# Opening transfers in another order: the transform weights first, the first feed-forward matrix behind the reads of Z, the second one in quarters behind a later read

## The chip, the cores and the metric

The kernel runs on one core of a Trainium2 chip. The core has five engines that run side by side, each through its own list of instructions in order: TensorE (PE, matrix products), VectorE (DVE), ScalarE (ACT), GpSimd (POOL) and SyncE (SP). They wait for one another through semaphores. Copies between the chip's DRAM and the on-chip memory SBUF are carried by 16 DMA engines. An engine issues such a transfer as one instruction of its own list; in this kernel SP issues most of them, POOL issues the loads of `x` and of `moe_w_out`. The profile shows the transfers of SP as queue q1 (hardware_dynamic) and those of POOL as queue q0 (software_dynamic). The metric is the device time of one execution in microseconds (us); lower is better.

## The reference

A spectral layer over 8 sequences of 3008 positions and 256 features is followed by a feed-forward block on all 24064 rows:

```python
X = np.fft.rfft(x, axis=1)                    # x: 8 x 3008 x 256
Xr, Xi = X.real, X.imag
Yr = Xr @ w_r - Xi @ w_i + b_r                # w_r, w_i: 256 x 256
Yi = Xr @ w_i + Xi @ w_r + b_i
Yr = np.sign(Yr) * np.maximum(np.abs(Yr) - 0.01, 0.0)      # likewise Yi
y = np.fft.irfft(Yr + 1j * Yi, n=3008, axis=1)
h = y.reshape(-1, 256) @ moe_w_in             # 256 x 2048
g = np.where(h > 0.0, h, np.exp(np.minimum(h, 0.0)) - 1.0)
out = g @ moe_w_out                           # 2048 x 256
```

## The kernel before

A transform of length 3008 is done as two smaller ones, 47 and 64 points, in units named by letters. For one batch `b`:

- A (`unit_A`, 6 of them) multiplies the loaded `x` (three tiles `xt0` to `xt2`) by the matrix `M1` and stores the result to a DRAM buffer `DA`. `load_Z` reads `DA` back in another arrangement, as tile `Z`.
- X (`unit_X`, 8) multiplies `Z` by `M2` into `XT`.
- M (`m_group`, called by `unit_M` or, in the opening, `first_M`; 12) applies `w_r` and `w_i`, adds the bias and shrinks by 0.01. The weights were cast before, by four instructions on POOL, into `wcat_r` and `wcat_s`.
- B (`unit_B`, 6) goes back by `M3` and stores to a DRAM buffer `DB`. `load_Bs` reads that back as four tiles `Bs`.
- Y (`unit_Y`, 8) multiplies `Bs` by `M4` into `yT`.
- `front` and `back` are the feed-forward block: `front` multiplies by `w_in_s` into `hps`, ACT and DVE form the ELU into `gT`, and `back`, two steps later, multiplies by `w_out_r` into `ps_o`. One batch has 48 such steps, one step takes two of the 16 column blocks of `moe_w_in`, so eight steps in a row go through all of `moe_w_in` and `moe_w_out`.

The order of all instructions is written out by hand. The opening does batch 0 alone through A, X, M, B, with filler products (`idle_pe`) on TensorE; then come the A units of batch 1 and the first two Y units of batch 0. After that the main loop runs 384 steps, and `plan` puts the units of the next batches between the steps: in batch 0 the Y units 2 to 5 stand ahead of `front` in steps 1 to 4, and the X units of batch 1 from step 5 on. A unit that stands there ahead of `front` runs ahead of it in the order of TensorE too.

What the opening loads, and in which order, before the change:

- POOL issues the six loads of `x` for batch 0 (line 115) from the very start, between the instructions that build index tables.
- SP issues the six stores of `DA`, then `w_r` and `w_i` (lines 504 and 505), the four reads of `Z`, the two bias rows, and the first quarter of `moe_w_in` (`load_w_in(0)`, line 580; the transfer itself is line 564). That last one writes into memory that the constants' staging tiles (`stagep`, among them `w_r_f` and `w_i_f`) held until then, so it waits for the last reader of those.
- POOL, in its own list, casts the weights (lines 506 to 509), then runs `gate(Z_of[0][:, 8, 0:1])`. `gate` is a copy of one column into a small tile: it does nothing but make POOL wait until that part of its source has landed, and with it all that POOL issues later. Behind it stand the three loads of `x` for batch 1 and both halves of `moe_w_out` (lines 584 and 585, transfer line 569).
- SP's `load_w_in(1)`, `(2)` and `(3)` stand behind the stores of units B 0, 1 and 2 (lines 613, 617, 621).
- At the end of the opening SP issues `load_Bs(0, 0)` and `(0, 1)` (lines 635 and 636), which wait for all stores of `DB`; between the A units of batch 1 come their three stores of `DA` (line 156) and the other two reads of `Bs`; then the two reads of `Z` for batch 1 (line 655), which wait for those stores.

`scale_w_in` (lines 646 to 653) turns each quarter of `moe_w_in` into its bf16 form behind the opening, on DVE and ACT.

Of the kernel before, what the change touches and what calls it, by code (L numbers as in the profile page):

```python
# [29 lines left out]
def kernel(  # L30
# [11 lines left out]
    nc = tc.nc  # L42
    P = nc.NUM_PARTITIONS
# [6 lines left out]
    NFT = DFF // P  # L50
# [54 lines left out]
    Bs_of = {}  # L105
    yT_of = {}
    def load_x(b, ci, m0=0, m1=8):

        src = bass.AP(
            tensor=x.tensor,  # L110
            offset=x.offset + (b * S + 8 * ci + m0) * D,
            ap=[[N1 * D, N2], [(NJ - 1) * D, 2], [D, m1 - m0], [1, D]],
        )
        dst = xts[ci][:, m0:m1, :]
        nc.gpsimd.dma_start(dst, src.bitcast(F32R))
# [98 lines left out]
    def first_M(q, i, eng):  # L214

        ps = pre1.tile([P, 2 * D], F32, name="mps1", tag="mps1")
        yb, clip = m_group(0, q, i, ps[:])
        let_go()
        Y_ = Y_of[0, q][:, i, :]
        if eng is nc.scalar:  # L220
            nc.scalar.activation(clip[:], yb[:], AF.Relu, bias=lam_n[:])
            held.append((Y_, yb, clip))
        else:
            eng.tensor_scalar(clip[:], yb[:], LAM, -LAM, ALU.min, ALU.max)
            eng.tensor_tensor(Y_, yb[:], clip[:], ALU.subtract)
# [35 lines left out]
    def load_Bs(b, w):  # L261

        Bs = wk4.tile([4 * K1, 8, D], BF16, name="Bs", tag="Bs")
        dv = DB_of[b].rearrange("k (c h m) d -> (k c h) m d", c=2, h=2)
        nc.sync.dma_start(Bs[:], dv[:, 8 * w : 8 * w + 8, :])
        Bs_of[b, w] = Bs
# [32 lines left out]
    with tc.tile_pool(name="stagep", bufs=1) as stagep:  # L299
# [29 lines left out]
        def row(name, shape):  # L329
            return stagep.tile(shape, F32, name=name)  # L330
# [3 lines left out]
        w3, a3 = (wk2.tile([P, NV, N2], F32, name="A", tag="A") for _ in range(2))  # L334
        w_r_f = row("w_r_f", [P, 2, D])
        w_i_f = row("w_i_f", [P, 2, D])


        nc.scalar.activation(dume[:], busy[:, 0:1], AF.Sin, bias=0.0, scale=0.0)

# [145 lines left out]
        def fA(u):  # L486
            unit_A(0, u, alone=True)
            if u < 5:
                idle_pe(3)
# [11 lines left out]
        wraps(1)  # L501
        signs(0)
        fA(5)
        nc.sync.dma_start(w_r_f[:], w_r.rearrange("(c p) e -> p c e", p=P))
        nc.sync.dma_start(w_i_f[:], w_i.rearrange("(c p) e -> p c e", p=P))
        pool.tensor_copy(wcat_r[:, :, 0:D], w_r_f[:])
        pool.tensor_copy(wcat_r[:, :, D : 2 * D], w_i_f[:])
        pool.tensor_scalar(wcat_s[:, :, 0:D], w_i_f[:], -1.0, None, ALU.mult)
# [50 lines left out]
    def load_w_in(q):  # L559
        if q < 3:  # L560
            wf = late3.tile([P, 2, FQ], F32, name="w_in_f", tag="Et")
        else:
            wf = late2.tile([P, 2, FQ], F32, name="w_in_f", tag="osb")
        nc.sync.dma_start(wf[:], w_in_v[:, :, q * FQ : q * FQ + FQ])
        w_in_f.append(wf)

    def load_w_out(hh):
        hf = slice(hh * NFT // 2, (hh + 1) * NFT // 2)
        nc.gpsimd.dma_start(w_out_r[:, hf, :], w_out_v[:, hf, :])

    def gate(src):

        t = gatep.tile([P, 1], F32, name="gate", tag="gate")
        nc.gpsimd.tensor_copy(t[0 : src.shape[0], :], src)


    def fB(v, on_dve=False):
        unit_B(0, v, alone=True, on_dve=on_dve)

    load_w_in(0)  # L580
    gate(Z_of[0][:, 8, 0:1])
    for ci in range(3):
        load_x(1, ci)
    load_w_out(0)
    load_w_out(1)
    for u in range(8):
        unit_X(0, u, alone=True, on_dve=u in (1, 4, 7))
        if u == 1:
# [21 lines left out]
    first_M(1, 1, nc.scalar)  # L610
    first_M(2, 0, nc.gpsimd)
    fB(0)
    load_w_in(1)
    first_M(2, 1, nc.scalar)
    first_M(3, 0, nc.gpsimd)
    fB(1)
    load_w_in(2)
    first_M(3, 1, nc.scalar)
    first_M(4, 0, nc.gpsimd)
    fB(2)  # L620
    load_w_in(3)
    first_M(4, 1, nc.scalar)
    first_M(5, 0, nc.scalar)
    fB(3)
# [9 lines left out]
        )  # L634
    load_Bs(0, 0)
    load_Bs(0, 1)

    def scale_w_in(q, on_dve):
        dst = w_in_s[:, :, q * FQ : q * FQ + FQ]
        if on_dve:  # L640
            nc.vector.tensor_scalar_mul(dst, w_in_f[q][:], 2.0 / S)
        else:
            nc.scalar.activation(dst, w_in_f[q][:], AF.Copy, scale=2.0 / S)
# [232 lines left out]
```

## Time and profile before

| what | value |
|---|---|
| time, median of 3 runs | 930.38 us (930.08 to 931.6) |
| profiled execution, its own time | 931.51 us |
| its span, first to last instruction | 929.7 us |
| mean granted TensorE clock | 0.998 of full speed |
| TensorE busy | 909.2 us, 98% of the span |
| VectorE, ScalarE, GpSimd busy | 734.5, 710.7 and 267.9 us |
| share of the chain that ended last on TensorE | 75% |
| moved by DMA | 106.21 MB, 114 GB/s over the span |
| moved by DMA from 4 to 15 us of the span | 353 GB/s |

Times in the views are counted from the start of the span. "Busy" counts instructions that compute; a wait is charged to what released it. The chain that ended last is followed back from the last instruction: each piece is the work that released the next one. In the table of stretches each row gives, for each engine, its busy time and the number of its instructions, then the granted TensorE clock, the mean busy share of the 16 DMA engines (a share above 1 means that the packets of several queues overlapped) and the rate in GB/s. "SPq" and "POOLq" are the instructions with which SP and POOL issue transfers.

### The profile page before, as it was taken

What the parts mean: (1) busy time and instruction counts of PE and PEld (TensorE: products, weight loads), DVE (VectorE), ACT (ScalarE), POOL (GpSimd) and SP (SyncE); (2) the same over time, 40 slices, a digit from 0 to 9 for tenths busy, and PEclk for the clock granted to TensorE, in tenths of its full rate; (3) what the DMA queues carried; (4) which work ended last, traced back from release to release, by engine and by line L of the source; (5) the groups of instructions that cost most, each with busy time, mean ns of one, the idle gap of its engine ahead of it and who ended that gap; (6) DMA issues with size and microseconds to landing.
All of it is one profiled execution on the core that took longest, in us unless ns stands there. A gap on an engine that the chain in (4) does not pass through costs nothing.

```text
span 929.7 us, 16768 instructions
## 1 busy us (share of the span) xinstructions
PE 909.2 (98%) x6583; PEld 644.4 (69%) x6583; DVE 734.5 (79%) x863; ACT 710.7 (76%) x818; POOL 267.9 (29%) x352
## 2 busy tenths in 40 slices
PE   8879999999999999999999999999999999999997
PEld 3447677776677666776677766777667766677775
DVE  7868778877788767886778877887778876888997
ACT  6657887787878788688787878778787878676654
POOL 6801441133310431205412153113331043321332
PEclk9999999999999999999999999999999999999999
DMA  8984216621383224722166021752138002421011
GB/s 264 353 254 136 91 47 187 196 69 46 95 223 111 69 65 126 224 84 86 51 181 202 24 91 46 222 161 68 47 94 224 22 24 63 116 51 43 23 46 43
DMA packets 90655, 106.21 MB, mean 114 GB/s; under 512 B 5264, under 2 KB 81296, under 8 KB 87216
## 3 DMA queue, kind: packets, MB, share of 16 engines
q1 hardware_dynamic: 84320, 77.61, 29.8%
q0 software_dynamic: 5968, 27.26, 8.9%
q8 instruction: 51, 0.84, 0.4%
q10 hardware_dynamic: 288, 0.26, 0.1%
q14 instruction: 28, 0.23, 0.1%
HBM read 55.31 MB, written 49.81 MB: 113 GB/s over the span
## 4 chain that ended last, share of the span: by engine, by line
PE 75%; DVE 14%; DMA 4%; ACT 4%; issue 1%; SPq 1%; DVEq 0%; POOL 0%; ACTq 0%; POOLq 0%
PE ps_o L749 30%; PE hps L688 29%; PE mps L189 8%; DVE gT L713 8%; DVE Et L724 3%; PE bps L238 2%; PE aps L143 2%; PE xps L174 2%; DMA Z<-DA 2%; DVE gT L715 1%; PE yps L276 1%; ACT Et L701 1%; DMA DA<-A 1%; DVE Et L726 1%; DMA xt<-in_x_dram 1%
## 5 line engine op out<-in xcount | busy, mean ns | idle before, releaser
L749 PE MATMUL ps_o<-w_out_r,gT 128*128 128x256 f32 (+1 forms) x3072 | 485.8, 301 | 0.8 <-DVE gT L713 0.5
L749 PEld LDWEIGHTS ps_o<-w_out_r,gT 128*128 128x128 f32 (+1 forms) x3072 | 406.4, 186 | 65.5 <-DVE gT L713 14.4
L688 PE MATMUL hps<-yT,w_in_s 128*128 128x512 bf16 (+1 forms) x1536 | 390.5, 376 | 5.4 <-DVE gT L715 2.7
L701 ACT ACTIVATE Et<-hps 128x1024 f32<-128x1024 f32 (+1 forms) x299 | 301.4, 1008 | 84.4 <-PE hps L688 80.4
L713 DVE SCALAR_TENSOR_TENSOR gT<-Et,hps 128x1024 fp32r<-128x1024 f32 (+2 forms) x187 | 219.9, 1176 | 62.9 <-ACT Et L699 41.6
L715 DVE SCALAR_TENSOR_TENSOR gT<-hps,Et 128x1024 fp32r<-128x1024 f32 (+1 forms) x198 | 240.1, 1213 | 17.6 <-DVE Et L726 0.9
L688 PEld LDWEIGHTS <-w_in_s 128*128 128x128 bf16 x1536 | 131.8, 98 | 141.0 <-issue 24.0
L726 DVE TENSOR_SCALAR Et<-Et 128x1024 f32<-128x1024 f32 (+1 forms) x198 | 136.0, 687 | 58.0 <-ACT Et L701 51.4
L204 POOL TENSOR_SCALAR clip<-yb 128x512 f32<-128x512 f32 x84 | 51.7, 615 | 335.1 <-DVE yb L196 234.5
L724 POOL TENSOR_SCALAR Et<-Et 128x512 f32<-128x512 f32 (+1 forms) x102 | 64.3, 630 | 271.1 <-ACT Et L701 269.9
L698 ACT ACTIVATE Et<-hps 128x1024 f32<-128x1024 f32 x84 | 86.4, 1029 | 70.0 <-PE hps L688 70.0
L205 POOL TENSOR_TENSOR Y<-yb,clip 128x512 bf16<-128x512 f32 x84 | 107.3, 1278 | 7.0
L196 DVE TENSOR_TENSOR yb<-mps,bias_bc 128x512 f32<-128x512 f32 x96 | 65.7, 687 | 39.3 <-PE mps L189 32.4
L699 ACT ACTIVATE Et<-Et 128x1024 f32<-128x1024 f32 x84 | 88.8, 1058 | 2.7
L126 ACT CAST yT<-yps 128x752 bf16<-128x752 f32 x63 | 49.7, 788 | 13.4 <-PE yps L276 13.4
L126 ACT CAST XT<-xps 128x768 bf16<-128x768 f32 x61 | 49.1, 807 | 13.7 <-PE xps L174 13.7
L189 PE MATMUL mps<-wcat_r,XT 128*128 128x512 bf16 x192 | 58.1, 384 | 0.6 <-ACT XT L126 0.6
L189 PE MATMUL mps<-wcat_s,XT 128*128 128x512 bf16 x192 | 57.1, 379 | 0.0
L126 ACT CAST A<-aps 128x1024 bf16<-128x1024 f32 x45 | 45.5, 1013 | 14.3 <-PE aps L143 11.9
L724 DVE TENSOR_SCALAR Et<-Et 128x512 f32<-128x512 f32 (+1 forms) x102 | 55.6, 545 | 0.4 <-ACT Et L701 0.2
L189 PEld LDWEIGHTS <-XT 128*128 128x128 bf16 x384 | 30.3, 98 | 29.5 <-ACT XT L126 0.9
L763 ACT COPY osb<-ps_o 128x512 f32<-128x512 f32 x88 | 47.2, 587 | 2.8 <-PE ps_o L749 2.8
(103 smaller groups left out, 398.5 us busy)
## 6 DMA issues: line engine op xcount, KB each, us to landing
xt<-in_x_dram POOLq DMA_DIRECT2D x21, 1024.0 KB, 5.2
out_dram<-osb SPq DMA_DIRECT2D x158, 128.0 KB
Bs<-DB SPq DMA_DIRECT2D x32, 384.0 KB
DA<-A SPq DMA_DIRECT2D x21, 512.0 KB
DB<-Bz SPq DMA_DIRECT2D x21, 512.0 KB
Z<-DA SPq DMA_DIRECT2D x7, 1152.0 KB
Z<-DA SPq DMA_DIRECT2D x11, 384.0 KB
xt<-in_x_dram POOLq DMA_DIRECT2D x6, 512.0 KB, 6.4
```

What stands on the lines that cost most here:

```text
L126: nc.scalar.copy(dst, src)
L189: nc.tensor.matmul(ps, lhsT=XT[:, dt, c, o : o + P], rhs=wm[:, dt, :], start=(m == 0 and dt == 0), stop=(m == 1 and dt == 1),)
L205: nc.gpsimd.tensor_tensor(Y_of[b, q][:, i, :], yb[:], clip[:], ALU.subtract)
L688: nc.tensor.matmul(hps[:, s, 0:nb], lhsT=w_in_s[:, dt, ft * P : ft * P + P], rhs=yT[:, dt, bs : bs + nb], start=(dt == 0), stop=(dt == 1),)
L698: nc.scalar.activation(E_, hps[:, :, 0:nb], AF.Relu, scale=-1.0)
L699: nc.scalar.activation(E_, E_, AF.Exp, scale=-1.0)
L701: nc.scalar.activation(E_, hps[:, :, 0:nb], AF.Exp)
L713: nc.vector.scalar_tensor_tensor(o, e, -1.0, h, ALU.add, ALU.max)
L715: nc.vector.scalar_tensor_tensor(o, h, 0.0, e, ALU.max, ALU.add)
L724: eng.tensor_scalar(E_[:, s], E_[:, s], 1.0, 0.0, ALU.min, ALU.max)
L726: nc.vector.tensor_scalar(E_, E_, 1.0, -1.0, ALU.min, ALU.add)
L749: nc.tensor.matmul(po[q][0 : t1 - t0, i_ % 2, :], lhsT=gT[:, s, t0:t1], rhs=w_out_r[:, ft, :], start=(ft == 0 and i_ % 2 == 0), stop=(ft = ...
```

## The change

Four moves, all of them transfers; no computing instruction is added or taken away, except one `gate`.

1. `w_r` and `w_i` are issued by SP at the very top, ahead of the stores of `DA`. The four casts on POOL stay where they are in POOL's list.
2. All four quarters of `moe_w_in` are issued where only the first was: on SP, behind the reads of `Z` and the bias.
3. Both halves of `moe_w_out` leave their place behind the loads of `x` for batch 1. In their stead four quarters are issued by POOL behind a new `gate` on the first read of `Bs`, at the end of the opening.
4. Nothing stands any more between the stores of `DB` on SP.

```diff
         w_r_f = row("w_r_f", [P, 2, D])
         w_i_f = row("w_i_f", [P, 2, D])
-
+        nc.sync.dma_start(w_r_f[:], w_r.rearrange("(c p) e -> p c e", p=P))
+        nc.sync.dma_start(w_i_f[:], w_i.rearrange("(c p) e -> p c e", p=P))
...
         fA(5)
-        nc.sync.dma_start(w_r_f[:], w_r.rearrange("(c p) e -> p c e", p=P))
-        nc.sync.dma_start(w_i_f[:], w_i.rearrange("(c p) e -> p c e", p=P))
         pool.tensor_copy(wcat_r[:, :, 0:D], w_r_f[:])
...
     def load_w_out(hh):
-        hf = slice(hh * NFT // 2, (hh + 1) * NFT // 2)
+        hf = slice(hh * NFT // 4, (hh + 1) * NFT // 4)
         nc.gpsimd.dma_start(w_out_r[:, hf, :], w_out_v[:, hf, :])
...
-    load_w_in(0)
+    for q in range(4):
+        load_w_in(q)
     gate(Z_of[0][:, 8, 0:1])
     for ci in range(3):
         load_x(1, ci)
-    load_w_out(0)
-    load_w_out(1)
...
     fB(0)
-    load_w_in(1)
...
     fB(1)
-    load_w_in(2)
...
     fB(2)
-    load_w_in(3)
...
     load_Bs(0, 0)
     load_Bs(0, 1)
+    gate(Bs_of[0, 0][:, 0, 0:1])
+    for q in range(4):
+        load_w_out(q)
```

## The prediction

> **What bounds the kernel now.** I read the chain that ended last first. From 75 us on it is TensorE, step after step, to the end (the page: PE 75% of the chain, 98% busy), and no transfer of the opening is waited for there. So whatever the change does is decided by when TensorE gets through the first 75 us, and those I read from the same chain, piece by piece (start, length, what):
>
> ```profile
> 2.18 6.01 DMA xt<-in_x_dram
> 15.62 3.09 DMA DA<-A
> 19.66 5.80 DMA Z<-DA
> 48.78 4.03 DMA DB<-A
> 55.95 2.44 SPq L265
> 58.47 6.16 DMA DA<-A
> 65.07 10.00 DMA Z<-DA
> ```
>
> The opening hangs on transfers at both its ends: `x` in, `DA` out, `Z` in; then computing from 27 to 48 us; then `DB` out, SP's issues, batch 1's `DA` out and its `Z` in. The last piece ends at 75.07, where X unit 2 of batch 1 starts. The longest waits up to 80 us say the same:
>
> ```profile
> PE yps L276 <- DMA Bs<-DB: 2.2, 1, 2.2
> PE xps L174 <- DMA Z<-DA: 1.6, 3, 0.7
> ```
>
> Then SP's own list, for what each transfer stands behind:
>
> ```profile
> 16.02 0.55 SPq L504 DMA_DIRECT2D w_r_f<-in_w_r_dram  x1
> 24.61 0.38 SPq L564 DMA_DIRECT2D w_in_f<-in_moe_w_in_dram  x1
> 52.88 0.79 SPq L265 DMA_DIRECT2D Bs<-DB  x2
> 58.47 1.00 SPq L156 DMA_DIRECT2D DA<-A  x1
> 64.71 0.77 SPq L163 DMA_DIRECT2D Z<-DA  x2
> ```
>
> And the table of stretches, for what the DMA engines carry (last two columns: busy share, GB/s):
>
> ```profile
> 38.00:44.00 6.00, 6.00 (x45) 2.59 (x40) 5.25 (x9) 3.96 (x5) 5.57 (x6) 1.00 1.64 349
> 51.00:54.00 3.00, 3.00 (x13) 1.35 (x14) 2.56 (x4) 1.96 (x3) 0.00 (x0) 1.00 0.15 37
> 54.00:58.00 4.00, 1.56 (x20) 0.81 (x18) 1.13 (x2) 1.08 (x2) 0.00 (x0) 1.00 0.96 268
> 58.00:64.00 6.00, 4.36 (x25) 2.24 (x26) 2.86 (x4) 3.29 (x5) 0.00 (x0) 0.72 1.09 341
> 64.00:66.00 2.00, 2.00 (x21) 1.66 (x20) 1.66 (x3) 1.34 (x2) 0.00 (x0) 1.00 0.17 43
> 66.00:72.00 6.00, 6.00 (x56) 4.77 (x52) 5.42 (x6) 5.08 (x6) 0.00 (x0) 1.00 0.97 247
> ```
>
> The reader is to see that from 54 to 64 the DMA engines are full, and with what: four `Bs` of 0.39 MB and three `DA` of 0.52 MB, 3.14 MB; the rows give 4 x 268 + 6 x 341 = 3.12 MB. These ten microseconds lie on the chain. The change puts `moe_w_out` (2.10 MB) into them.
>
> **Move 1, `w_r` and `w_i` first.** Two SP issues (0.55 and 0.49 us) leave the stretch from 16.0 to 17.1, where SP waits anyway (until 18.71) for the last `DA`: removing them gives SP nothing. Their 0.52 MB stood behind that `DA` in the same queue; its 3.09 us may shorten by 0 to 0.4, I take 0. At the top SP is free from 0.7 us, and data starts about 1.1 us after an issue (`Bs`: issued 52.88, 37 GB/s until 54), so the weights flow from about 1.9. `x` starts at 2.5 and then paces all six A units: its loads land at 5.5, 8.2, 9.4, 10.8, 12.2 and 13.7 us, the A products start at 5.57, 8.23, 9.58, 10.93, 12.27 and 13.81. At the full 353 GB/s of the stretch from 4 to 15 us the weights are 1.5 us of DMA time; before 4 us only 134 GB/s run (2.5 to 4), so most of it fits into room that was empty. Bounds 0 and 1.5; I take 0.4, nearer the empty rows. The casts on POOL (0.93, 0.61, 3.09, 0.61 us; 19.45 to 24.58 now) may start at 13.1. Their user starts at 28.97 and waited for `XT`, so this gives nothing, and the index work on DVE beside which they now fall has 0.5 us or more to spare before `Z` lands (22.55).
>
> **Move 2, `moe_w_in`.** SP's first such issue waited until 24.61 for the casts; now it waits only for DVE's last staging read (22.65), and four issues (0.38 to 0.54 us each) go out where SP has nothing to do before 37.77. They stand behind the `Z` reads in the same queue. The loads of `x` for batch 1 leave POOL's gate at about 24.3, when the second `Z` lands, not 25.17: they may cost the last `Z` 0 to 0.4 us; I take 0, since its data were through about 1 us ahead of its landing at 26.97, and `x` needs as long from issue to data. 2.1 MB and 3.1 MB of `x` at 391 GB/s (28 to 37 us) end near 39 us. `moe_w_in` is read from 48.67, `x` from 47.34: both are in time.
>
> **Move 3a, the stores of `DB` are freed.** Now each stands among half-megabyte loads; the DMA engines run full (365 GB/s) from 44 to 51, and the last store takes 4.03 us. With the queue empty it takes about as long as the last `DA` of batch 0, equally 0.26 MB: 3.09. With 0.75 us at 349 GB/s for the bytes, 1.1 to the first byte and 1 to 1.6 behind the last one (data end near 51.2, landing 52.8), it is 2.85 to 3.45. Gain 0.6 to 1.2; I take 0.8. `Bs` is then issued at 52.88 + 0.4 - 0.8 = 52.5 and lands at 56.5 instead of 56.87.
>
> **Move 3b, `moe_w_out` in the full stretch.** POOL has nothing to do from 45.4 to 75, so the gate (0.18 to 0.49 us) and four issues (half of the 1.10 and 1.13 us of the halves) cost it nothing, and nothing else waits behind them. Data flow from about 57.8. By then SP's queue has moved 4.2 x 268 = 1.13 MB; 2.02 MB of `Bs` and `DA` are left, which before ended at 64.0. The nearest row for the two queues together is 38 to 44 us: 349 GB/s, and there `moe_w_out`'s rest and SP's `DB` and `moe_w_in` got about the same each. At equal shares 2.02 + 2.10 MB end together near 57.8 + 11.8 = 69.6, and `moe_w_out` displaces at most 2.10 / 349 = 6.0 us. If SP's queue kept four fifths, `DA` would be late by 1.3 us, `moe_w_out` would fill the nearly empty rows 64 to 66 and 72 to 75, and the rest would fall on `Z`: some 2 us in all. Bounds 2 and 6.0; near the equal share, with some of the end falling into the gap behind the last `DA`, I take 5.0. The `Z` reads follow only when the last `DA` has landed (64.63 now), so all of it goes on to X unit 2, which had no slack (it waited 0.7 us).
>
> A sentence beside it: the Trainium skill, DMA: Bandwidth & Descriptors, Anatomy of one DMA, fits a transfer issued from GpSimd as 2.0 us plus its bytes at 436 GB/s, which makes the 2.10 MB an estimated 4.8 us instead of 6.0 and the sum +4.4 instead of +4.6; no row of this trace with both queues busy is that fast (349).
>
> Is `moe_w_out` itself late? The first `back` runs at 64.46 and needs the first quarter, the third at 68.8 the second. At half of 349 the quarters land near 61.5, 64.5, 67.5 and 70.5; the last two are read later than 72. Hidden, with 2 us or more to spare.
>
> **Sum.** +0.4 (start) - 0.8 (`DB`) + 5.0 (`moe_w_out` before `Z`) = +4.6 us at X unit 2, and from there on TensorE carries it to the end. The profiled execution is 931.51 us (span 929.7 and 1.8 around it), so 936.1 against it; it lies 1.1 above the median of the runs, and against that median of 930.38 I forecast 935.0.
>
> **Rivals.**
>
> Faster, by the place of `moe_w_out` alone: it yields to SP's queue. For it: 64 to 66 and 72 to 75 us are nearly empty (43 and 14 GB/s) and could hold 0.6 + 1.0 MB; POOL's loads are issued later than the first two `Bs` and the first `DA`. Against it: from 38 to 44 the same matrix was not held back by SP's transfers. It decides where less than 0.4 / 5.0 of the matrix, 0.17 MB, moves ahead of the last `DA` or of `Z`. With the best ends of the other terms (start 0, `DA` -0.4, `DB` -1.2) it gives 1.6 to 2.5 us less: 928.3.
>
> Half hidden: SP keeps the larger share, the displacement is at its bound of 2, the sum +1.6, and the time 932.0. Only the four-to-one share that I have assumed speaks for it.
>
> Slower still: TensorE's clock falls a second time. In the row from 58.70 to 62.40 it was granted 0.55, after two waits of TensorE of 2.2 and 1.0 us. With the change TensorE comes to X unit 0 at about 69.5 and `Z`'s first part lands up to 5.2 us (64.71 to 69.92, no wait) behind an issue at 69.7, so it idles 3 to 5 us. The same 3.7 us at 0.55 cost 1.7; with the start at its bound (+1.1) it is +7.4, 937.8. Against it: the slow steps lie beneath the wait for `Z`'s second part. The Trainium skill, TensorE: Matmul & The Clock Gate, Part 1, has the clock halve after one idle window of about 3.4 us; by that rule the longer wait would be enough by itself, and here the two shorter waits sufficed already.
>
> **How the numbers follow.** Forecast (+2.5 to +6.5): 0.54. Slower still (+6.5 to +9): 0.12. Half hidden (0 to +2.5): 0.14, of which 0.08 above 0.2%. Faster rival: 0.20, of which 0.14 beyond 0.2%. Here 0.2% is 1.9 us, about what a measurement of this kernel can tell from no change. So slower 0.54 + 0.12 + 0.08 = 0.74, within 0.12, faster 0.14. The range leaves out most of the faster rival and the tail of the slowest: 930.3 to 938.5; the forecast's own range is 932.9 to 936.9.
>
> **What the profile after would show.** Start: the first A products at 5.6 to 6, the sixth at 14.2; much more, and the weights collide with `x`. `DB`: the last store lands about 3.1 us after its issue. The main step: rates near 350 GB/s from 58 to 69, the last `DA` landing at 69 to 70 instead of 64.6, the reads of `Z` issued there, TensorE waiting for `Z` ahead of two X units, X unit 2 at about 79.7. If the last `DA` lands by 65, the step on the shared DMA engines is wrong, and so is the forecast. A wait of TensorE on `w_out_r` would show that the quarters come too late, which I exclude.

## The result, and the profile after

| | before | changed |
|---|---|---|
| median on the same chip | 931.03 us (930.08 to 931.97) | 937.16 us (935.58 to 938.34) |
| ratio, 95% interval | | 1.0066 [1.0053, 1.0078] |
| profiled execution, its time | 931.51 us | 936.45 us |
| its span | 929.7 us | 934.7 us |
| X unit 2 of batch 1 starts at | 75.11 us | 79.83 us |
| from there to the end of the span | 854.6 us | 854.9 us |

The change makes the kernel slower by 6.1 us. Measured once more (e14 below), it came to 1.0076 [1.0064, 1.0087]. Everything is lost before X unit 2 of batch 1: in all 14 profiled executions of this study the way from there to the end of the span takes 854.6 to 855.0 us.

The chain that ended last, of the changed kernel, up to that point (start, length, what):

```profile
1.46 6.07 DMA xt<-in_x_dram
17.36 2.31 DMA DA<-A
20.60 6.43 DMA Z<-DA
56.08 2.66 SPq L265
58.84 12.04 DMA DA<-A
71.32 8.47 DMA Z<-DA
79.83 0.52 PE xps L174 x8
```

Against the chain of before: the last store of batch 1's `DA` took 6.16 us and now takes 12.04. The reads of `Z` behind it are shorter, 8.47 instead of 10.00. The wait for the last store of `DB` is no longer in the chain. SP's list and POOL's, of the changed kernel, show what stands beside that store:

```profile
53.13 0.79 SPq L265 DMA_DIRECT2D Bs<-DB  x2
58.84 1.17 SPq L156 DMA_DIRECT2D DA<-A  x1
70.96 1.72 SPq L163 DMA_DIRECT2D Z<-DA  x2
```

```profile
57.21 0.18 POOL L573 CAST gate<-Bs 96x1 f32<-96x1 bf16 x1 [10.22 <-DMA Bs<-DB]
57.34 3.09 POOL L568 DMA_DIRECT2D w_out_r<-in_moe_w_out_dram  x4
```

SP issues `Bs` and `DA` at nearly the same times as before (52.88 and 58.47), and `Z` 6.25 us later (64.71 before). In between stands `moe_w_out`. The table of stretches, changed kernel (last three columns: granted clock, busy share of the DMA engines, GB/s):

```profile
58.00:64.00 6.00, 3.44 (x28) 1.80 (x28) 3.54 (x5) 3.83 (x5) 2.42 (x4) 1.00 1.21 342
64.00:66.00 2.00, 0.30 (x2) 0.00 (x0) 1.75 (x2) 1.02 (x1) 0.00 (x0) 1.00 1.45 265
66.00:71.00 5.00, 4.22 (x24) 3.33 (x25) 1.31 (x2) 0.96 (x2) 0.00 (x0) 0.66 1.32 328
```

The DMA engines are full up to 71 instead of 64, and the rate is (6 x 342 + 2 x 265 + 5 x 328) / 13 = 325 GB/s. TensorE stands idle in the second row, and is granted less clock in the third. Its three longest waits in the first 100 us, changed kernel (us in total, times, longest):

```profile
PE xps L174 <- DMA Z<-DA: 3.0, 5, 1.0
PE ps_o L747 <- DMA w_out_r<-in_moe_w_out_dram: 2.5, 1, 2.5
PE aps L143 <- DMA xt<-in_x_dram: 2.2, 1, 2.2
```

Of the 3.0 us in the first line 1.5 are waits for batch 1's `Z`, 0.9 ahead of X unit 0 and 0.6 ahead of X unit 2; the rest are for batch 0's. The middle line was not there before: the first `back` waited 2.5 us for the first quarter of `moe_w_out`, which landed 9.4 us behind its issue. The last line, 0.4 before, is the first `x`, late by the weights ahead of it.

### The profile page after: what moved, and what is told of

Read it like the earlier page. It is cut to its first block, busy times and chain, and to the rows that moved or that the text cites. A ratio compares the mean times of both kernels' runs of the same rounds, so it can differ in the third digit from the quotient of the medians.

```text
span 934.7 us, 16664 instructions
## 1 busy us (share of the span) xinstructions
PE 904.8 (97%) x6477; PEld 645.9 (69%) x6583; DVE 734.6 (79%) x863; ACT 710.5 (76%) x818; POOL 267.7 (29%) x355
## 4 chain that ended last, share of the span: by engine, by line
PE 75%; DVE 14%; ACT 4%; DMA 4%; issue 2%; SPq 0%; DVEq 0%; POOL 0%; ACTq 0%; POOLq 0%
PE ps_o L747 30%; PE hps L686 28%; PE mps L189 8%; DVE gT L711 8%; DVE Et L722 3%; PE bps L238 2%; PE aps L143 2%; PE xps L174 2%; DMA Z<-DA 2%; DMA DA<-A 2%; DVE gT L713 1%; ACT Et L699 1%; PE yps L276 1%; DVE Et L724 1%; DMA xt<-in_x_dram 1%
## 5 line engine op out<-in xcount | busy, mean ns | idle before, releaser
L686 PE MATMUL hps<-yT,w_in_s 128*128 128x512 bf16 (+1 forms) x1463 | 384.1, 376 | 9.1 <-DVE gT L713 2.7
L699 ACT ACTIVATE Et<-hps 128x1024 f32<-128x1024 f32 (+1 forms) x299 | 301.4, 1008 | 84.2 <-PE hps L686 76.8
L189 PE MATMUL mps<-wcat_s,XT 128*128 128x512 bf16 x183 | 55.2, 379 | 1.1
L189 PE MATMUL mps<-wcat_r,XT 128*128 128x512 bf16 x171 | 53.6, 385 | 0.6 <-ACT XT L126 0.6
```

The lines of the kernel that those rows point to most:

```text
L189: nc.tensor.matmul(ps, lhsT=XT[:, dt, c, o : o + P], rhs=wm[:, dt, :], start=(m == 0 and dt == 0), stop=(m == 1 and dt == 1),)
L686: nc.tensor.matmul(hps[:, s, 0:nb], lhsT=w_in_s[:, dt, ft * P : ft * P + P], rhs=yT[:, dt, bs : bs + nb], start=(dt == 0), stop=(dt == 1),)
L699: nc.scalar.activation(E_, hps[:, :, 0:nb], AF.Exp)
```

## The experiments

Each kernel was timed in five rounds against the kernel before on the same chip. Times along the opening are from the one profiled execution of each (us); "Z landed" is the second part of batch 1's `Z`, seen at POOL's gate behind it.

| kernel | Bs issued | Z issued | Z landed | X unit 2 | ratio to before, 95% interval |
|---|---|---|---|---|---|
| before | 52.88 | 64.71 | 75.1 | 75.11 | 1 |
| changed | 53.13 | 70.96 | 79.8 | 79.83 | 1.0066 [1.0053, 1.0078] |
| changed, again (e14) | 54.65 | 72.45 | 81.4 | 81.41 | 1.0076 [1.0064, 1.0087] |
| move 1 alone (e1) | 53.40 | 65.13 | 73.7 | 75.35 | 1.0026 [1.0017, 1.0034] |
| move 2 alone (e2) | 53.45 | 65.30 | 75.4 | 75.47 | 1.0001 [0.9992, 1.0009] |
| move 3 alone (e3) | 51.93 | 70.34 | 79.3 | 79.81 | 1.0069 [1.0057, 1.0081] |
| moves 2 and 3 (e4) | 53.50 | 70.65 | 79.5 | 79.56 | 1.0064 [1.0052, 1.0076] |
| moves 1 and 3 (e11) | 53.23 | 71.52 | 80.1 | 80.11 | 1.0068 [1.0054, 1.0081] |
| changed, half of `moe_w_out` late (e5) | 52.30 | 68.10 | 76.8 | 78.14 | 1.0047 [1.0035, 1.0059] |
| changed, first quarter early, spare load (e7) | 57.02 | 75.48 | 84.6 | 86.61 | 1.0094 [1.0078, 1.0110] |
| the same with fillers (e8) | 52.30 | 69.73 | 78.1 | 78.12 | 1.0080 [1.0065, 1.0095] |
| before, `Bs` reads later, fillers (e10) | 52.19 | 61.70 | 71.5 | 73.83 | 1.0004 [0.9995, 1.0012] |
| move 1 with fillers (e12) | 52.97 | 64.74 | 74.0 | 74.37 | 0.9997 [0.9988, 1.0006] |
| e10, move 2, one quarter late (e13) | 52.00 | 64.11 | 73.8 | 73.80 | 1.0009 [1.0000, 1.0018] |

The theory after the result: `moe_w_out`'s bytes, put between the read of `Bs` and the read of `Z`, push `Z` back (move 3). The rivals: the wait of the first `back` for its quarter, and the half clock behind it; the weights ahead of `x` (move 1).

**Moves 2 and 3, without move 1 (e4).** Edit to the changed kernel:

```diff
-        nc.sync.dma_start(w_r_f[:], ...)      # at the top
-        nc.sync.dma_start(w_i_f[:], ...)
         fA(5)
+        nc.sync.dma_start(w_r_f[:], ...)
+        nc.sync.dma_start(w_i_f[:], ...)
         pool.tensor_copy(wcat_r[:, :, 0:D], w_r_f[:])
```

> The changed kernel with move 1 undone: w_r and w_i are issued behind the sixth A unit again. Theory (the weights ahead of the first x cost the opening about 2 us up to the last store of DB, and nothing swallows that, since no other transfer is in flight then): the first A products at 5.6 instead of 7.6, the last DB store issued near 48.8 instead of 50.8, Bs issued near 51.1 instead of 53.1, X unit 2 of batch 1 near 77.9 instead of 79.8: about 2 us less than the changed kernel, 3 us more than before (1.003). Rival (the late start is swallowed on the way, by the wait for moe_w_out or for Z): as the changed kernel, +5 us or more over before (1.0055).

Measured: 936.66 us, 1.0064. Undoing move 1 gives nothing back; the rival's number holds. The first A products did start at 5.83 again, but `Bs` was issued no earlier than in the changed kernel (53.50 against 53.13): in that execution the first `Z` landed 5.2 us behind its issue, and the X units ran at a granted clock of 0.50 from 26 to 28.

**Move 2 alone (e2).**

```diff
-    load_w_in(0)
+    for q in range(4):
+        load_w_in(q)
...
-    load_w_in(1)        # likewise (2) and (3)
```

> The kernel before with move 2 alone: all of moe_w_in behind the first reads of Z, everything else as before (moe_w_out still in halves behind x of batch 1). Theory (the gain in the changed kernel, where the last store of DB landed in 2.3 us instead of 4.0, comes from taking moe_w_in out from among those stores; the loss is moe_w_out's bytes ahead of batch 1's DA and Z): the last DB store is issued at about 48.8 and lands in 2.3 to 2.8, Bs is issued at 51.1 to 51.6 instead of 52.9, the last DA lands near 63.2 instead of 64.6, X unit 2 of batch 1 starts near 73.7 instead of 75.1, so about 1.2 to 1.8 us faster than before. Rival (the stores were held up by moe_w_out's tail, not by moe_w_in): no change, 0 +- 0.5 us.

Measured: 931.30 against 931.06 us, no change: the rival. The last store of `DB`, issued at 50.2, still had 3.3 us until `Bs` was issued: `moe_w_out`, which had ended by 44 in the kernel before, ran among the stores instead: 0.98 MB on POOL's queue from 44 to 50, 322 GB/s in all. The transfers only changed places.

**Half of the dose (e5).** Edit to the changed kernel:

```diff
         load_x(1, ci)
+    for q in range(2):
+        load_w_out(q)
...
     gate(Bs_of[0, 0][:, 0, 0:1])
-    for q in range(4):
+    for q in range(2, 4):
         load_w_out(q)
```

> The changed kernel with half of the dose: the first two quarters of moe_w_out stand behind x of batch 1 again, the last two stay behind the first read of Bs. Theory (its bytes push the last DA and with it Z of batch 1 back, about in proportion): 1.05 MB instead of 2.10 MB, the last DA lands near 68 instead of 71, X unit 2 near 77 instead of 79.8, TensorE no longer waits for w_out_r, about 2.7 us less than the changed kernel and 2.3 more than before (1.0025). Rival A (the first back's wait for its quarter and the half clock behind it make the loss): as TensorE does not wait for it any more, within 0.5 us of the time before, 1.000. Rival B (any transfer on the second queue at that place costs the whole, by its being there and not by its bytes): as the changed kernel, 1.0055.

Measured: 934.86 us, 1.0047, between all (1.0066) and nothing, and not by the wait for `moe_w_out`, which is gone. From the issue of `Bs` to that of `Z` it is 15.8 us; 11.8 before and 17.8 with all of it late. So half the bytes cost 4.0 us of the 6.0. The theory's direction holds, not its proportion (it had 1.0025): the second half counts less. A part of the reason shows in the changed kernel, where POOL's queue still moved 0.41 MB from 70 to 72 us while SP's moved 0.01: those bytes stood ahead of no `DA` any more. Here TensorE lost more than `Z` did: it waited 3.6 us at a stretch at X unit 0, its clock fell, and X unit 2 started 1.3 us behind the landing of `Z`.

**The same bytes, without the wait for them (e7).** Edit to the changed kernel:

```diff
         load_x(1, ci)
+    load_w_out(0)
...
     gate(Bs_of[0, 0][:, 0, 0:1])
-    for q in range(4):
+    spare = sparep.tile([P, NFT // 4, E], F32R, name="spare")
+    nc.gpsimd.dma_start(spare[:], w_out_v[:, 0 : NFT // 4, :])
+    for q in range(1, 4):
         load_w_out(q)
```

> The changed kernel with the same bytes in the same place, but without TensorE's wait for the first quarter: quarter 0 of moe_w_out is loaded behind x of batch 1, and in its old place behind the gate the same 0.52 MB go to a spare tile that nobody reads. Theory (bytes ahead of DA and Z decide, the wait for w_out_r is hidden beneath the wait for Z): TensorE does not wait for w_out_r and its clock does not fall at 67, yet the last DA lands at 71 and X unit 2 starts near 79.8 as in the changed kernel: 1.0055 of before, less than 0.7 us from the changed kernel. Rival (the late quarter and the half clock make the loss): X unit 2 near 76 and the time 2 to 4 us less than the changed kernel.

Measured: 939.3 us, 1.0094. The wait for the quarter is gone and the time is no better, rather worse. So that wait is not the loss, which refutes the rival; but the theory's number (as the changed kernel) is missed as well. The profile shows the reason. This kernel's table of stretches, behind the last `DA`:

```profile
74.00:80.00 6.00, 0.39 (x6) 0.39 (x7) 3.05 (x3) 0.00 (x0) 0.00 (x0) 0.87 0.92 244
80.00:84.00 4.00, 3.78 (x22) 2.99 (x21) 0.69 (x1) 1.82 (x2) 0.00 (x0) 0.50 0.55 141
84.00:87.00 3.00, 3.00 (x28) 2.24 (x26) 1.30 (x2) 1.82 (x2) 1.37 (x3) 0.78 0.28 44
```

TensorE no longer stops for `moe_w_out`, arrives early at X unit 0, waits there for `Z` 6.1 us at one stretch, and then runs at half clock: two steps take 4.0 and 3.0 us instead of 2.15 each, and X unit 2 starts 2.0 us behind the landing of `Z`. (This execution, 943.3 us, was the slowest of the six, and late from its opening, with `Bs` issued at 57.0; so its absolute times stand back.) The next kernel tests this.

**The same with fillers (e8).** 24 filler products ahead of X unit 0 in the main loop:

```diff
         if b == 0:
+            def warm(n):
+                ps = unit_ps("warm", False)
+                for _ in range(n):
+                    nc.tensor.matmul(ps[:, 0, :], lhsT=busy[:, 0:P], rhs=busy[:], start=True, stop=True)
+            f0[lead + 4].insert(0, (warm, (24,)))
             f1[xs[0]].append(...)
```

> The kernel with quarter 0 early and the spare load in its place, and now 24 filler products on TensorE ahead of X unit 0 of batch 1, where it waited 6.1 us for Z and then ran at half clock. Theory (the 2 us by which that kernel is slower than the changed one are the half clock behind this one long wait): TensorE keeps its clock at 1.00 behind X unit 0, a step there takes 2.15 us instead of 4.0 and 3.0, X unit 2 starts when the second part of Z lands, and the time is 1.5 to 2.5 us less than without the fillers: 1.0065 to 1.0075 of before. Rival (the extra loss is in the transfers): no change, 1.009 or more.

Measured: 937.44 us, 1.0080 [1.0065, 1.0095]. TensorE's list of this kernel (start, length, what):

```profile
73.84 0.50 PE L174 MATMUL xps<-M,Z 96*128 96x96 bf16 x8
75.97 0.52 PE L174 MATMUL xps<-M,Z 96*128 96x96 bf16 x8
78.12 0.52 PE L174 MATMUL xps<-M,Z 96*128 96x96 bf16 x8
```

The steps are 2.15 us and X unit 2 starts as `Z` lands (78.11): that the half clock made the steps long is shown. How much of the time it made, the medians do not tell well: six runs of this kernel spent 1.7 to 3.6 us outside the span from first to last instruction, all other kernels 1.7 to 1.9, and no run shows why. By the spans the fillers give 1.7 us: the median span is 6.5 us above that of the kernel before with them (934.75 against 928.3), 8.2 without (937.5 against 929.3). That is what the theory has, and the 6.5 is near the changed kernel's 6.1 and, again, 7.6: the same bytes without the wait for them cost about the same.

**Move 3 alone (e3).** The kernel before with the four quarters behind the first read of `Bs`:

```diff
-    load_w_out(0)
-    load_w_out(1)
...
     load_Bs(0, 1)
+    gate(Bs_of[0, 0][:, 0, 0:1])
+    for q in range(4):
+        load_w_out(q)
```

> The kernel before with move 3 alone: the four quarters of moe_w_out behind the first read of Bs, the weights and moe_w_in where they were. Theory (move 3 is the whole loss): from the issue of Bs to the issue of batch 1's Z about 17 to 18 us instead of 11.8, X unit 2 near 79.5, and the time 5.0 to 6.5 us over before, 1.0055 to 1.007, as the whole change. Rival (a part of the loss comes from the weights' or moe_w_in's new place): less than 4 us over before, below 1.0043.

Measured: 936.35 against 930.06 us, 1.0069, as forecast: move 3 alone is enough for the whole loss. `Z` is issued 18.4 us behind `Bs`, a little above the 17 to 18 expected.

**Move 1 alone (e1).**

```diff
         w_i_f = row("w_i_f", [P, 2, D])
+        nc.sync.dma_start(w_r_f[:], ...)
+        nc.sync.dma_start(w_i_f[:], ...)
...
         fA(5)
-        nc.sync.dma_start(w_r_f[:], ...)
-        nc.sync.dma_start(w_i_f[:], ...)
```

> The kernel before with move 1 alone: w_r and w_i at the very top, all else as before. Theory (they delay the first x by up to 2 us, but behind the computing of the opening the stores of DB still stand among moe_w_in's transfers, whose bytes end near 51 whenever the stores come, so most of it is swallowed there): the first A products 1 to 2 us later, the issue of Bs less than 1 us later, the time within 0.7 us of before (0.9995 to 1.001). Rival (nothing swallows it): Bs and X unit 2 later by 1.5 to 2 us, ratio 1.0015 to 1.002.

Measured: 932.03 us, 1.0026, 2.0 us more than before: the rival, not the theory, and more than the rival's number. By itself the move is paid in full, and not by way of `Z`: that landed at 73.7, but TensorE came to X unit 2 only at 75.35. Its list in the opening, of this kernel and then of the kernel before:

```profile
7.04 1.19 PE L143 MATMUL aps<-xt,M 128*128 128x512 f32 x2 [1.57 <-DMA xt<-in_x_dram]
8.03 1.50 PE L292 MATMUL ips<-busy 128*128 128x512 bf16 x3
8.97 1.42 PE L143 MATMUL aps<-xt,M 128*128 128x512 f32 x2
10.94 0.82 PE L143 MATMUL aps<-xt,M 128*128 128x512 f32 x2
```

```profile
5.60 1.19 PE L143 MATMUL aps<-xt,M 128*128 128x512 f32 x2
8.23 0.73 PE L143 MATMUL aps<-xt,M 128*128 128x512 f32 x2 [0.39 <-DMA xt<-in_x_dram]
```

The two products of a unit take 1.19 to 1.42 us until about 10 here, and before only the first did; at full clock they take 0.7 to 0.8. The wait for `x` of 1.57 us breaks the fillers' run, and TensorE stays slow through the second unit as well.

**Move 1 with more fillers (e12).** The kernel of move 1 alone, with the wait for the late `x` filled:

```diff
-    idle_pe(9)
+    idle_pe(16)
```

> The kernel before with move 1 alone and 7 more filler products on TensorE ahead of the first A unit, which cover its wait for the late x. Theory A (half of move 1's loss of 2.4 us is the half clock at which the A products run behind that wait): the clock stays at 1.00 up to 15 us, the sixth A unit starts near 14.2 instead of 14.9, ratio 1.0010 to 1.0018. Theory B (only the late x counts): as move 1 alone, 1.0022 to 1.0030.

Measured: 930.50 against 930.41 us, 0.9997: all of the 2 us is gone, more than theory A had allowed. TensorE's list of this kernel, cut to the window from 5 to 9 us:

```profile
4.41 3.08 PE L292 MATMUL ips<-busy 128*128 128x512 bf16 x9
7.13 0.82 PE L143 MATMUL aps<-xt,M 128*128 128x512 f32 x2
8.69 0.50 PE L143 MATMUL aps<-xt,M 128*128 128x512 f32 x1
```

The first unit runs at full speed although it starts no earlier than with move 1 alone (7.13 against 7.04), and the reads of `Z` of batch 0 are issued at 18.56 instead of 19.37 (18.79 before). So the gap that the half-megabyte opens on TensorE was most of its cost, not the bytes. With the gap filled the second to the sixth A unit start only 0.35 to 0.46 us later than before, and the last `DA`, which no longer has the weights behind it, makes that good: the reads of `Z` are issued 2.6 us behind it instead of 3.2. The kernel before with these fillers alone was not run; but there the second unit waits for `x` (0.39 us, in the list above), so that a faster first unit would have gained it nothing.

**Moves 1 and 3 (e11), and the changed kernel again (e14).** The edits of e1 and e3 together; and no edit at all.

> The kernel before with moves 1 and 3, moe_w_in in its old places. Move 1 alone measured 1.0026, move 3 alone 1.0069, all three moves 1.0066. Theory A (what move 1 loses in the opening is swallowed once move 3 makes TensorE wait for Z anyway, at the last stores of DB and beneath that wait): 1.0066 to 1.0075, as move 3 alone. Theory B (the two add up, and move 2 gives the 2 us back in the whole change, by freeing the stores of DB): 1.009 to 1.0098.

> The changed kernel itself beside the three others, as their measure on the same chip: 1.006 to 1.0075 of before.

Measured: 936.65 us, 1.0068, and 938.0 us, 1.0076. Move 1's 2 us do not appear on top of move 3 (1.0069 alone): theory A. In the profiles of move 3 without and with move 1, `Bs` is issued at 51.93 and 53.23, `Z` lands at 79.3 and 80.1, and X unit 2 starts at 79.81 and 80.11: the difference shrinks from 1.3 to 0.3 on the way. A part of this is clock. In the profile without move 1, TensorE was granted 0.50 from 76 to 78 and reached X unit 2 0.5 us behind the landing of `Z`; in the one with it, the clock stayed at 1.00, behind a wait at X unit 0 that was no shorter (2.15 us against 1.97). Why the one fell and the other did not, and whether other executions do the same, is left open.

**The other sign (e10).** The kernel before, relieved in the same stretch, with 8 more fillers ahead of the first Y unit:

```diff
-            load_Bs(0, 2 + u // 2)             # for u in (1, 3)
...
     scale_w_in(3, False)
+    load_Bs(0, 2)
     for s0, s1 in ((0, 8), (8, NS)):
         load_Z(1, s0, s1)
-    idle_pe(3)
+    load_Bs(0, 3)
+    idle_pe(11)
```

> The kernel before, with the same stretch relieved instead of loaded: the third read of Bs is issued behind the last store of DA of batch 1, the fourth behind the reads of Z, so 0.79 MB less stands ahead of the last DA; and 8 more filler products on TensorE ahead of the first Y unit, where its clock fell behind a wait of 2.2 us. Theory (bytes ahead of the last DA set when Z comes, here with the other sign): the issue of Z 1.5 to 2.3 us earlier than 64.7, no half clock from 58.7 to 62.4, X unit 2 near 73.0 instead of 75.1, 1.5 to 2.5 us faster, ratio 0.9973 to 0.9984. Rival (the reads of Z run in their own time or TensorE arrives no earlier): no change, 1.000.

Measured: 930.53 against 930.06 us, no change. The transfers did what the theory says: with 0.79 MB less ahead, `Z` was issued 9.5 us behind `Bs` instead of 11.8, 2.3 us for which 0.79 / 341 GB/s = 2.3, and it landed 2.4 us before TensorE came for it. But TensorE came at 73.83 and no earlier. The median of the kernel before puts its X unit 2 no later: 930.06 less the 1.8 us around the span and the 854.8 behind X unit 2 gives 73.5. So the dose with the other sign shows in the transfers, and not in the time.

**A last try (e13).** The kernel of e10 with move 2 and only the last quarter of `moe_w_out` late:

```diff
+    for q in range(4):
+        load_w_in(q)
...
+    for q in range(3):
+        load_w_out(q)
...
+    gate(Bs_of[0, 0][:, 0, 0:1])
+    load_w_out(3)
```

> The relieved kernel (third and fourth read of Bs later, 8 more fillers) with moe_w_in behind the first reads of Z and three quarters of moe_w_out in the old place; only the last quarter behind the first read of Bs. In the relieved kernel Z of batch 1 landed 2.4 us before TensorE came for it. Theory (that room takes the 0.52 MB, 1.5 us, and the stores of DB, now with less beside them, land 1 us sooner, which brings Bs and with it TensorE forward): Bs issued near 51.3, X unit 2 near 73.0, ratio 0.998 to 0.9995 of before. Rival (the transfers only change places, as with moe_w_in alone): 1.000 or above.

Measured: 931.35 us, 1.0009: the rival. `Bs` was issued at 52.00 rather than 51.3, and the quarter took 2.6 us of the room (12.1 from `Bs` to `Z`, against 9.5). X unit 2 started at 73.80, 0.1 us behind where TensorE comes anyway (2.15 us a step from X unit 1 at 71.55). None of these kernels beats the kernel before.

## Why the prediction was right

It forecast 935.0 (930.3 to 938.5), slower by its main step; measured were 937.16 and, again, 938.0. The forecast's own range of +2.5 to +6.5 us holds the measured +6.1, not the +7.6 of the repeat; as times, 937.16 and 938.0 both lie above its 936.9 and inside the wider range. The mechanism is the one named: move 3 by itself makes the loss (e3), it grows with the bytes (e5, and in the transfers of e10 with the other sign), and with `Z` everything behind shifts. X unit 2, forecast at about 79.7, started at 79.83. The terms behind that number, by the two profiles:

- *Start, +0.4 (bounds 0 and 1.5).* At the issue of the last `DA` of batch 0 it is +1.7 (17.36 against 15.62), at the last store of `DB` +2.0. Mis-sized, beyond its bound, and for a reason that the step did not contain: it counted bytes, and their 0.4 is about right once the gap on TensorE is filled (0.35 to 0.46 in e12). That most of the rest is the clock behind that gap is shown for move 1 alone (e1, e12). In the whole change the term does not show in the time (e4, e11).
- *The last `DA` of batch 0, 0 (0 to -0.4):* it took 2.31 instead of 3.09 us, so -0.8; outside the bound. Until the reads of `Z` behind it are issued it is 2.4 to 2.8 us in seven of the eight profiles with the weights at the top, and 3.1 to 3.5 in the six with the weights behind it.
- *Stores of `DB`, -0.8 (0.6 to 1.2):* from the last store's issue to that of `Bs` 4.1 us before, 2.4 after, -1.7. Outside the bounds too: the 3.09 us taken as the price without other traffic was itself a store with the weights behind it. And 4.1 is one execution, not the rule: in e10, whose transfers are the same up to there, the last store was issued at 49.85, when the loads were ending (247 GB/s from 49 to 50, 122 from 50 to 51), and `Bs` followed 2.3 us behind. Start and stores together were to bring `Bs` 0.4 earlier; it was issued 0.25 later.
- *`moe_w_out`, +5.0 (2 to 6.0):* 11.8 became 17.8 us from `Bs` to `Z`, +6.0, the upper bound. From 58 to 71 SP's queue moved 2.19 MB and POOL's 2.02, together 325 GB/s and not 349. So the equal shares came out over the whole stretch, but not within it: POOL's first bytes moved near 60.9, 3.5 us behind the issue where 1.1 had been taken from `Bs`, and from 66 to 70 POOL's queue moved 0.90 MB and SP's 0.39. That the two cancel is luck.
- *`moe_w_out` itself in time, "which I exclude":* wrong. The first quarter was to land 4 us behind its issue and took 9.4, of which 3.5 passed before its first bytes moved; TensorE waited 2.5 us. It cost nothing by itself, being hidden beneath the wait for `Z` (e7, e8).
- *The reads of `Z`, unchanged:* 10.4 us became 8.9.

The late start could be seen before the change, in the row from 38 to 44 that the step on `moe_w_out` took its rate and its shares from. There POOL's queue moved 1.56 MB and SP's 0.52, not about the same each: the store of `DB` issued at 37.77 moved its first bytes after 41.5, and till then POOL's queue ran alone. Kernel before, from 38 to 39 and then from 42.5 to 43 (packets, MB, share of the 16 engines):

```profile
q0 software_dynamic: 341, 0.35, 192.6%
```

```profile
q1 hardware_dynamic: 181, 0.10, 75.7%
q0 software_dynamic: 67, 0.06, 47.7%
```

From 42 to 43 both moved, 0.16 MB each, at 309 and 330 GB/s in the two halves of that microsecond, close to the 325 of the changed kernel. The first line also shows that a busy share above 1 does not need two queues.

So +0.25 + 6.0 - 1.5 = +4.7 at X unit 2 against a sum of +4.6: near agreement, by errors that cancel, and so by luck. The medians moved by 6.1. The median lies 2.2 us above the forecast of 935.0: 0.65 because the kernel before measured 931.03 beside the changed one and not 930.38, the other 1.5 because the kernels differ by 6.1 and not by 4.6. For most of that the last term has a place. The reads of `Z` take 8.4 to 10.1 us in all twelve other profiled executions and 8.9 in the changed kernel; the 10.4 of the kernel before is the longest. TensorE's list of that kernel, X units 1 and 2:

```profile
72.07 0.52 PE L174 MATMUL xps<-M,Z 96*128 96x96 bf16 x8
75.11 0.51 PE L174 MATMUL xps<-M,Z 96*128 96x96 bf16 x8 [0.74 <-DMA Z<-DA]
```

At 2.15 us a step TensorE by itself would have come to X unit 2 at 74.2, so `Z` made it 0.9 us late in that execution, and from 74.2 to the 79.83 of the changed kernel it is 5.6. "X unit 2, which had no slack" was read from that one execution, and that it was 1.1 us above the median was taken off the forecast as an offset common to both. It need not be common: it can sit in the very step that the sum took over unchanged. The medians of before put X unit 2 at 73.5 to 74.5 (e10 and e13 have it at 73.8), those of the changed kernel at 80.6 to 81.4. That the ordinary execution of before hardly waits for `Z` is inferred from the medians and those two kernels, not seen in a trace; and the profiled execution of the changed kernel is itself 0.7 us below its median, for a reason that no run shows.

The rivals: the faster one falls, `moe_w_out` did not yield; once its bytes moved, it got the larger share. Half hidden falls with it. Of the slowest one the clock did fall a second time, as the row from 66 to 71 shows, but behind the wait for `moe_w_out` and not behind that for `Z` at X unit 0, which was 0.9 us and not 3 to 5; and its slow steps lay beneath the wait for `Z`, as was held against it. In e7, where TensorE waited 6.1 us in one piece, it did cost time.

## What to carry to other kernels

A transfer that is moved out of a stretch with room must be followed to where it lands: here the same 2.1 MB cost 6 us less among the computing than in a stretch where nearly every byte stood ahead of a store, a read and the next product. Where a rate or a share for two queues is taken from a row, look first whether both moved in that row. Before taking over a wait of one profiled execution as a step of a sum, compare that execution with the median: what it has more of is in one of its steps, and a step that was slow by chance need not be slow again. And a late input can cost more by the clock that TensorE loses in the gap than by its lateness; a few filler products tell the two apart.

## What the runs showed of the hardware

- The two queues together moved less than POOL's queue nearly alone. From 58 to 71 us, with a busy share of 1.2 to 1.45, 325 GB/s went through; from 28 to 37 in the kernel before, with 3.30 of 3.52 MB on POOL's queue, 391, and from 38 to 39, with POOL's queue alone, 349. The four quarters of 0.52 MB landed 9.4, 11.0, 12.4 and 13.1 us behind their issues. The Trainium skill, DMA: Bandwidth & Descriptors, Anatomy of one DMA, would give an estimated 2.0 us plus 1.2 for one of them; its fit does not hold here, beside a full second queue.
- A transfer issued while the other queue had the DMA engines full moved no byte for some time: POOL's quarter behind SP's queue 3.5 us in the changed kernel and 3.3 to 4.3 in the seven others with two or more pieces late, 2.2 to 2.7 in e13; SP's store behind POOL's queue at 37.77 in the kernel before about 4. Once both moved, from 66 to 69, they moved about as many packets in each microsecond (206 to 214 and 207 to 212); POOL's were of about 1 KB and SP's of 0.5 KB, so that POOL's queue got two thirds of the bytes.
- TensorE's clock fell in the changed kernel behind a wait of 2.5 us: idle from 64.3 to 66.78, with waits of 0.6 and 0.9 us in the three microseconds before, and at 0.50 from 67 to 70. The Trainium skill, TensorE: Matmul & The Clock Gate, Part 1, names an idle window of about 3.4 us; here shorter ones sufficed, and the measurement decides. The length of one wait does not settle it: behind 1.97 us the clock was 0.50 from 76 to 78 in e3, behind 2.15 us it stayed at 1.00 in e11.
- At the start of the span the granted clock is shown as 1.00 while the products run slow: the nine fillers of the kernel before take 0.45 us each from 1.45 on, later ones 0.27. Where the column shows 0.50 they take 0.50 each (three in 1.50 us from 9.86 in the changed kernel). So at the start the length of a product tells more of the clock than the column.
- A store of 0.26 MB with little other traffic took 2.3 to 2.4 us until the next transfer could be issued, at three places (last `DA` of batch 0 and last `DB` of the changed kernel, last `DB` of e3).
